# Expert steps in two parts, each with a pair of arms of its own

## The chip, the cores and the metric

The kernel runs on one core of a Trainium2 chip. Its engines are TensorE (PE: products, and PEld for the loads of weights ahead of them), VectorE (DVE), ScalarE (ACT), GpSimd (POOL) and SyncE (SP, which issues most of the DMAs). Each engine has an instruction stream of its own, read by a sequencer (PEldq, ACTq, DVEq, SPq in the rows); the streams meet by semaphores. The metric is the device time of one execution in microseconds, as the median of the runs.

## The reference, cut to what matters

Three layers follow each other. The experts at the end are what the change touches; the two ahead of them are only named here.

```python
def reference(**kwargs):
    ...
    attn_out = _attn_ref(**attn_kwargs)      # 4 x 8 heads, 576 tokens, D = 64
    x = ...                                  # 2304 tokens x 512
    x = _moe_ref(x=x, **moe_kwargs)          # relu(x @ w_in) ** 2 @ w_out, 512 -> 2048 -> 512
    return _moe2_ref(x=x, **moe2_kwargs)

def _moe2_ref(x, expert_emb, tau, w1, w2):
    ...
    expert_idx = np.argmax(logits, axis=1)   # one of 8 experts for each token
    ...
    for e in range(E):
        mask = expert_idx == e
        if not mask.any():
            continue
        h = np.maximum(x[mask] @ w1[e], 0.0)            # 512 -> 1024
        out[mask] = gate_w[mask, None] * (h @ w2[e])    # 1024 -> 512
    return out.astype(np.float32)
```

Which tokens belong to which expert is known only on the chip, at run time.

## The kernel before, in words

Attention comes first, then the dense layer, then the routing, which sorts the tokens by expert into blocks of 128 and writes a table: which expert each step uses, and some words whose bit s-1 holds a flag of step s. Then come the experts, from about 720 us on.

**Steps.** The experts run in steps of 256 tokens (two blocks), all for one expert. The program holds NST = 17 of them; steps 0 to 8 always run, later ones only while there are tokens left (L1342 to L1345). With these inputs 11 run, 0 to 10. Every product is made of three in fp32r, with hi and lo parts of both operands, so a step has 152 products on TensorE: four groups of layer 1 with 24 products each (`layer1(g)`, into a bank psh, L1249), four groups of layer 2 with 12 each (`layer2(g)`, into psy, L1265 to L1267), and 8 transposes of the tokens of the next step (`turned`, pst, L965). The order is that at the end of `body` (L1269 to L1291). Behind each layer1 group ScalarE writes hh (L1251) and VectorE hl (L1252), which layer2 of the group reads. The second half of a layer2 group stands under a small If on the word "half" (L1257), which skips it in a last, half-filled step.

**Weights.** An expert's weights are 8 pieces: 0 to 3 of w1, 4 to 7 of w2. SyncE loads them raw into x1[j] (L992 and L995; tile x in the rows), ScalarE casts a piece into Wh (L110) and VectorE computes the rest into Wl (L111). There are two slots of Wh and Wl, and a new expert takes the slot that the expert before it doesn't use. `own(j)` casts pieces 4 to 7 of the step's expert, `ahead(j)` pieces 0 to 3 of the next step's, each under an If on whether the expert changes there.

**Arms.** The slot of a step is known only at run time. So `arms` (L1293 to L1301) writes the body twice, once for slot 0 and once for slot 1, under an If and an Else on the step's bit of the word "odd"; TensorE, ScalarE and VectorE each choose on their own, by two ALU operations and a compare-and-branch (L1296 in the rows). An engine that takes the first arm ends it with a jump over the second. The choice falls to slots 0, 1, 1, 0, 0, 1, 1, 0, 0, 1 in steps 1 to 10. Within the arms the order on TensorE, ScalarE and VectorE is as written.

**Around the arms.** `block(s)` issues, behind the arms: the loads of pieces 4 to 7 on SyncE under an If on the word "more" (L1313), those of pieces 0 to 3 under another (L1316), and the gathers of the tokens of step s + 2 on POOL (L1205). `store` then multiplies psy by the gate on VectorE (L1326) and scatters the rows on POOL (L1327). In the rows, "issue" is idle time that no semaphore explains.

Of the kernel before, what the change touches and what calls it, by code (L numbers as in the profile page):

```python
# [19 lines left out]
ENG = mybir.EngineType  # L20
# [595 lines left out]
class Mlp:  # L616
# [46 lines left out]
    def layer1(self, hf, cc, f):  # L663
        nc, st, sh = self.tc.nc, self.st, self.sh
        if f == 0 and self.at == 0:
            later, self.later = self.later, at_once
            self.split_chunk(hf, cc)
            self.later = later
        xh, xl = self.xs[cc]
        self.turns += 1  # L670
        if self.psr is not None and self.turns % 2:
            ps = self.psr.tile([128, 512], F32, name="ps", tag="xt", bufs=2)
        else:
            ps = self.psm.tile([128, 512], F32, name="ps", tag="L1", bufs=1)
        ops = []
        for kc in range(4):
            fo = (f % 2) * 512 + kc * 128
            wh = sh.Wh[hf][f // 2][:, fo:fo + 128]
            wl = sh.Wl[hf][f // 2][:, fo:fo + 128]
            ops += [(wh, xh[kc]), (wh, xl[kc]), (wl, xh[kc])]  # L680
        for n, (a, b) in enumerate(ops):
            nc.tensor.matmul(ps[:, :CH], a, b, start=n == 0, stop=n == len(ops) - 1)  # L682
        r = st.tile([128, CH], F32, name="r", tag="r")
        gh = st.tile([128, CH], F32R, name="gh", tag="gh")
        gl = st.tile([128, CH], F32R, name="gl", tag="gl")
        self.later(1, "act", lambda: nc.scalar.activation(r, ps[:, :CH], AF.Relu))  # L686
        if self.square is nc.scalar:
            self.later(1, "act", lambda: nc.scalar.activation(r, r, AF.Square))
        else:
            self.later(2, "dve", lambda: nc.vector.tensor_tensor(r, r, r, ALU.mult))  # L690
        self.later(3, "act", lambda: nc.scalar.copy(gh, r))  # L691
        self.later(3, "dve", lambda: nc.vector.tensor_tensor(gl, r, gh.bitcast(F32), ALU.subtract))  # L692
        self.gT[hf, cc, f] = (gh, gl)
# [480 lines left out]
def experts(tc, sh, gates, w1, w2, out):  # L1174
    nc = tc.nc
    T = sh.T
    with ExitStack() as ctx:
# [36 lines left out]
        words = {}  # L1214

        def new(s):

            return words["once"] if s == 1 and "change" not in words else bit(words["change"], s)

        def load(js, s):  # L1220

            ev = nc.values_load(T.meta[0:1, s:s + 1], engines=[ENG.SP], min_val=0, max_val=E - 1)
            for j in js:
                load_expert_dyn(nc, sh, j, w1, w2, ev)

        def body(s, slot):


            Wh, Wl = sh.Wh[slot], sh.Wl[slot]
            hT = {}  # L1230

            def own(j):
                if s:
                    with tc.If(new(s) > 0):
                        piece(nc, sh, slot, j)

            def ahead(*js):
                if s + 1 < NST:
                    with tc.If(new(s + 1) > 0):
                        for j in js:  # L1240
                            piece(nc, sh, 1 - slot, j)

            def layer1(g):
                ps = new_bank().rearrange("p (a b) -> p a b", a=2)
                for a in range(2):
                    sl = slice((2 * g + a) * 128, (2 * g + a) * 128 + 128)
                    for kc in range(4):
                        for j, (w, x) in enumerate(((Wh, hi), (Wh, lo), (Wl, hi))):
                            nc.tensor.matmul(ps[:, a], w[kc][:, sl], x[:, kc], start=kc + j == 0, stop=kc + j == 5)  # L1249
                hh, hl = hT[g] = new_hh(), new_hl()  # L1250
                nc.scalar.activation(hh, ps, AF.Relu)  # L1251
                nc.vector.scalar_tensor_tensor(hl, ps, 0.0, hh.bitcast(F32), ALU.max, ALU.subtract)  # L1252

            def layer2(g):
                hh, hl = hT[g]
                for h in range(2):
                    with tc.If(bit(words["half"], s) < 1) if s and h else nullcontext():  # L1257
                        half(g, h, hh, hl)

            def half(g, h, hh, hl):  # L1260

                for a in range(2):
                    wh, wl = Wh[4 + g][:, a * 512:a * 512 + 512], Wl[4 + g][:, a * 512:a * 512 + 512]
                    xh, xl = hh[:, a, h * 128:h * 128 + 128], hl[:, a, h * 128:h * 128 + 128]
                    nc.tensor.matmul(y[h], xh, wh, start=g + a == 0, stop=False)  # L1265
                    nc.tensor.matmul(y[h], xh, wl, start=False, stop=False)  # L1266
                    nc.tensor.matmul(y[h], xl, wh, start=False, stop=g + a == 4)  # L1267

            own(4)  # L1269
            layer1(0)  # L1270
            own(5)
            layer1(1)
            own(6)
            own(7)
            if s == 0:
                words["once"] = nc.values_load(T.once[0:1], engines=[ENG.Activation, ENG.DVE], min_val=0, max_val=1)
            ahead(0)
            ahead(1)
            layer2(0)
            layer2(1)  # L1280
            layer1(2)
            ahead(2)
            layer1(3)
            ahead(3)
            layer2(2)
            if s + 1 < NST:
                for h in range(2):
                    turned(nc, sh, pst[h], h)
            if s == 0:
                next(gates)  # L1290
            layer2(3)  # L1291

        def arms(s, flag, *does):  # L1293

            kept = [list(r) for r in rings]
            with tc.If(bit(words[flag], s) < 1) as cmp, tc.manual_schedule(engines=IN_ORDER | {ENG.PE}):  # L1296
                does[0]()
            for r, was in zip(rings, kept):
                r[:] = was
            with cmp.Else(), tc.manual_schedule(engines=IN_ORDER | {ENG.PE}):  # L1300
                does[1]()  # L1301

        def block(s):
            if s == 0:
                body(0, 0)
                words["odd"] = word(0, [ENG.PE, ENG.Activation, ENG.DVE])
                words["change"] = word(1, [ENG.Activation, ENG.DVE])
                words["more"] = word(2, [ENG.SP])
                words["half"] = word(3, [ENG.PE])
            else:  # L1310
                arms(s, "odd", lambda: body(s, 0), lambda: body(s, 1))
            if s:
                with tc.If(bit(words["more"], s) > 0):  # L1313
                    load(range(4, 8), s)
            if s + 1 < NST:
                with tc.If(bit(words["more"], s + 1) > 0):  # L1316
                    load(range(4), s + 1)
            gather(s + 2)
# [132 lines left out]
```

## Time and profile before

| | |
|---|---|
| median of 3 runs | 982.22 us (979.92 to 982.36) |
| the profiled execution's own time | 982.79 us |
| its span, first to last instruction | 981.0 us |
| mean granted TensorE clock | 0.975 |
| busy: VectorE / ScalarE / POOL | 617.7 / 530.0 / 282.3 us |
| code fetched by DMA in the whole execution (q8) | 65 packets, 1.06 MB |

The span is that of the profiled execution; 982.79 - 981.0 = 1.8 us lie around it. TensorE's share stands with the other rows below. [...] Rows of a line give the count, the shortest, median and longest duration in ns, and the first and last start; where durations are far apart, single windows tell which one was long. A row of a window has its start and end, its length, the busy time (and count) of PE, PEld, DVE, ACT and POOL, the granted clock, the busy share of the DMA engines and GB/s. Sequencer operations (ALU, compare, branch) aren't counted as busy time; they show up only as rows of their line, and as idle time of the engine where the sequencer comes late.

### The profile page before, as it was taken

What the parts mean: (1) busy time and instruction counts of PE and PEld (TensorE: products, weight loads), DVE (VectorE), ACT (ScalarE), POOL (GpSimd) and SP (SyncE); (2) the same over time, 40 slices, a digit from 0 to 9 for tenths busy, and PEclk for the clock granted to TensorE, in tenths of its full rate; (3) what the DMA queues carried; (4) which work ended last, traced back from release to release, by engine and by line L of the source; (5) the groups of instructions that cost most, each with busy time, mean ns of one, the idle gap of its engine ahead of it and who ended that gap; (6) DMA issues with size and microseconds to landing.
All of it is one profiled execution on the core that took longest, in us unless ns stands there. A gap on an engine that the chain in (4) does not pass through costs nothing.

```text
span 981.0 us, 19093 instructions
## 1 busy us (share of the span) xinstructions
PE 919.5 (94%) x6271; PEld 791.1 (81%) x6271; DVE 617.7 (63%) x1761; ACT 530.0 (54%) x1387; POOL 282.3 (29%) x351
## 2 busy tenths in 40 slices
PE   7887788799999999999999999999999999999983
PEld 6666666688888888898888988888899889988963
DVE  4697778756676665488617778889753535353651
ACT  3676677677676766576655555665322323232430
POOL 4363554533333443000211111442312211111111
PEclk8899989899999999999999999999999999999997
DMA  7566655454444430155311112411062526252611
GB/s 167 134 175 152 155 141 133 102 127 96 115 96 116 96 87 2 65 169 155 108 44 44 64 46 90 157 66 54 22 216 66 195 85 185 88 161 85 180 40 34
DMA packets 107080, 105.79 MB, mean 108 GB/s; under 512 B 66095, under 2 KB 76335, under 8 KB 106944
## 3 DMA queue, kind: packets, MB, share of 16 engines
q1 hardware_dynamic: 101200, 90.17, 33.3%
q0 software_dynamic: 4544, 13.67, 4.4%
q8 instruction: 65, 1.06, 0.4%
q14 instruction: 71, 0.58, 0.2%
q10 hardware_dynamic: 1200, 0.30, 0.2%
HBM read 70.80 MB, written 14.70 MB: 87 GB/s over the span
## 4 chain that ended last, share of the span: by engine, by line
PE 74%; DVE 9%; issue 7%; DMA 4%; ACT 3%; POOL 2%; SPq 1%; POOLq 0%; ACTq 0%; DVEq 0%
PE ps L682 17%; PE psh L1249 11%; PE y L716 6%; PE y L718 5%; PE y L717 5%; PE xo L532 4%; PE ps L433 4%; PE pt L399 4%; PE psy L1267 3%; PE psy L1265 3%; PE psy L1266 3%; DMA raw<-in_moe_w_in_dram 2%; PE pt L401 2%; PE xo L511 1%; DVE x L819 1%
## 5 line engine op out<-in xcount | busy, mean ns | idle before, releaser
L682 PE MATMUL ps<-xh,Wh 128*128 128x256 f32 x416 | 120.0, 288 | 0.0
L394 POOL TENSOR_SCALAR A<-A,sm,g 128x512 f32<-128x512 f32 (+4 forms) x108 | 75.4, 706 | 152.0 <-DVE sm L457 58.2
L682 PE MATMUL ps<-xl,Wh 128*128 128x256 f32 x416 | 118.2, 284 | 0.9 <-DVE xl L656 0.9
L682 PE MATMUL ps<-xh,Wl 128*128 128x256 f32 x416 | 117.9, 283 | 0.0
L716 PE MATMUL y<-Wh,gh 128*128 128x512 f32 x288 | 115.3, 400 | 0.0
L718 PE MATMUL y<-Wh,gl 128*128 128x512 f32 x288 | 113.7, 395 | 0.1
L717 PE MATMUL y<-Wl,gh 128*128 128x512 f32 x288 | 113.4, 394 | 0.0
L1251 ACT ACTIVATE hh<-psh 128x512 fp32r<-128x512 f32 x44 | 26.3, 598 | 154.5 <-PE psh L1249 102.0
L1249 PE MATMUL psh<-xTh,Wh 128*128 128x256 f32 x352 | 101.0, 287 | 9.0 <-issue 8.8
L448 ACT ACTIVATE A<-A,nm 128x256 f32<-128x256 f32 (+2 forms) x144 | 80.2, 557 | 38.5 <-DVE nm L440 37.5
L1249 PE MATMUL psh<-xTl,Wh 128*128 128x256 f32 x352 | 99.9, 284 | 0.0
L1249 PE MATMUL psh<-xTh,Wl 128*128 128x256 f32 x352 | 99.9, 284 | 0.0
L440 DVE CUSTOM_DVE_ANT_0 A<-ps,mask 64x256 f32<-64x256 f32 (+4 forms) x160 | 75.5, 473 | 36.9 <-PE ps L433 34.4
L692 DVE TENSOR_TENSOR gl<-r,gh 128x256 fp32r<-128x256 f32 x144 | 69.8, 485 | 44.2 <-ACT gh L691 39.6
L1252 DVE SCALAR_TENSOR_TENSOR hl<-psh,hh 128x512 fp32r<-128x512 f32 x44 | 30.4, 690 | 103.8 <-ACT hh L1251 46.3
L686 ACT ACTIVATE r<-ps 128x256 f32<-128x256 f32 x144 | 54.8, 380 | 75.2 <-PE ps L682 67.6
L682 PEld LDWEIGHTS ps<-xh,Wh 128*128 128x128 f32 x416 | 79.6, 191 | 4.7 <-issue 1.9
L682 PEld LDWEIGHTS ps<-xl,Wh 128*128 128x128 f32 x416 | 79.7, 192 | 3.7 <-DVE xl L656 1.1
L682 PEld LDWEIGHTS ps<-xh,Wl 128*128 128x128 f32 x416 | 79.8, 192 | 0.0
L691 ACT CAST gh<-r 128x256 fp32r<-128x256 f32 x144 | 58.4, 406 | 37.4 <-PE y L717 35.3
L1249 PEld LDWEIGHTS psh<-xTh,Wh 128*128 128x128 f32 x352 | 67.6, 192 | 12.2 <-issue 11.5
L1249 PEld LDWEIGHTS psh<-xTl,Wh 128*128 128x128 f32 x352 | 67.6, 192 | 0.6
(330 smaller groups left out, 2440.1 us busy)
## 6 DMA issues: line engine op xcount, KB each, us to landing
x<-in_moe_w_dram SPq DMA_DIRECT2D x48, 512.0 KB, 5.0
raw<-in_moe_w_in_dram SPq DMA_DIRECT2D x16, 512.0 KB, 4.6
raw<-in_moe_w_out_dram SPq DMA_DIRECT2D x16, 512.0 KB, 3.8
ks<-hk SPq DMA_DIRECT2D x60, 128.0 KB, 2.4
x2d<-x SPq DMA_DIRECT2D x18, 256.0 KB, 2.0
kn<-in_k_dram SPq DMA_DIRECT2D x32, 128.0 KB, 3.7
vn<-in_v_dram SPq DMA_DIRECT2D x32, 128.0 KB, 3.2
x2p<-x SPq DMA_DIRECT2D x16, 256.0 KB, 2.5
```

What stands on the lines that cost most here:

```text
L394: nc.gpsimd.tensor_scalar(A, A, a, b, ALU.mult, ALU.mult)
L399: nc.tensor.transpose(out, A, ident)
L440: nc.vector.tensor_tensor_reduce(A[rows, a:n], tiles[j][rows, :w], mask[rows, end - w:end], -1.0, 3e38, ALU.add, ALU.min, nm[rows, j:j + 1])
L448: nc.scalar.activation(A[:, a:a + w], src, AF.Exp, bias=nm[:, 0:1], scale=sign, accum_out=sm[:, i:i + 1])
L682: nc.tensor.matmul(ps[:, :CH], a, b, start=n == 0, stop=n == len(ops) - 1)
L686: self.later(1, "act", lambda: nc.scalar.activation(r, ps[:, :CH], AF.Relu))
L691: self.later(3, "act", lambda: nc.scalar.copy(gh, r))
L692: self.later(3, "dve", lambda: nc.vector.tensor_tensor(gl, r, gh.bitcast(F32), ALU.subtract))
L716: nc.tensor.matmul(y, gh[:, sl], wh, start=first, stop=False)
L717: nc.tensor.matmul(y, gh[:, sl], wl, start=False, stop=False)
L718: nc.tensor.matmul(y, gl[:, sl], wh, start=False, stop=last)
L1249: nc.tensor.matmul(ps[:, a], w[kc][:, sl], x[:, kc], start=kc + j == 0, stop=kc + j == 5)
```

## The change

`body` gets a parameter `part`. Part 0 holds layer1(0), layer1(1), layer2(0), layer2(1) with own(4) to own(7), ahead(0) and ahead(1): 72 products. Part 1 holds the rest: layer1(2), layer1(3), layer2(2), the 8 transposes and layer2(3): 80 products. From step 1 on each part stands in a pair of arms of its own, so there are two choices on the word "odd" in each step, and the loads of pieces 4 to 7 are written between the two.

```diff
--- before.py
+++ after.py
@@ -1223,7 +1223,7 @@
             for j in js:
                 load_expert_dyn(nc, sh, j, w1, w2, ev)
 
-        def body(s, slot):
+        def body(s, slot, part):
 
 
             Wh, Wl = sh.Wh[slot], sh.Wl[slot]
@@ -1266,18 +1266,20 @@
                     nc.tensor.matmul(y[h], xh, wl, start=False, stop=False)
                     nc.tensor.matmul(y[h], xl, wh, start=False, stop=g + a == 4)
 
-            own(4)
-            layer1(0)
-            own(5)
-            layer1(1)
-            own(6)
-            own(7)
-            if s == 0:
-                words["once"] = nc.values_load(T.once[0:1], engines=[ENG.Activation, ENG.DVE], min_val=0, max_val=1)
-            ahead(0)
-            ahead(1)
-            layer2(0)
-            layer2(1)
+            if part == 0:
+                own(4)
+                layer1(0)
+                own(5)
+                layer1(1)
+                own(6)
+                own(7)
+                if s == 0:
+                    words["once"] = nc.values_load(T.once[0:1], engines=[ENG.Activation, ENG.DVE], min_val=0, max_val=1)
+                ahead(0)
+                ahead(1)
+                layer2(0)
+                layer2(1)
+                return
             layer1(2)
             ahead(2)
             layer1(3)
@@ -1302,16 +1304,17 @@
 
         def block(s):
             if s == 0:
-                body(0, 0)
+                body(0, 0, 0)
+                body(0, 0, 1)
                 words["odd"] = word(0, [ENG.PE, ENG.Activation, ENG.DVE])
                 words["change"] = word(1, [ENG.Activation, ENG.DVE])
                 words["more"] = word(2, [ENG.SP])
                 words["half"] = word(3, [ENG.PE])
             else:
-                arms(s, "odd", lambda: body(s, 0), lambda: body(s, 1))
-            if s:
+                arms(s, "odd", lambda: body(s, 0, 0), lambda: body(s, 1, 0))
                 with tc.If(bit(words["more"], s) > 0):
                     load(range(4, 8), s)
+                arms(s, "odd", lambda: body(s, 0, 1), lambda: body(s, 1, 1))
             if s + 1 < NST:
                 with tc.If(bit(words["more"], s + 1) > 0):
                     load(range(4), s + 1)
```

No computation changes its place on any engine. TensorE's stream shows what does. The first place is the middle of step 2, in the arm for slot 0, behind the last product of layer2(1); Wh0 and Wl0 are the weights of slot 0, Wh1 and Wl1 those of slot 1, psh0 to psh2 and psy0, psy1 the banks of the two layers. Before:

```order
L1265 MATMUL psy1_9341<-Wh0_5_76,hh1_9344 128x512
L1266 MATMUL psy1_9341<-Wl0_5_84,hh1_9344 128x512
L1267 MATMUL psy1_9341<-Wh0_5_76,hl1_9346 128x512
L1257 UNCONDITIONAL_BRANCH x2
L1249 MATMUL psh1_9336<-xTh_8044,Wh0_0_71 128x256
L1249 MATMUL psh1_9336<-xTl_8045,Wh0_0_71 128x256
L1249 MATMUL psh1_9336<-xTh_8044,Wl0_0_79 128x256
```

After:

```order
L1266 MATMUL psy1_9341<-Wl0_5_84,hh1_9344 128x512
L1267 MATMUL psy1_9341<-Wh0_5_76,hl1_9346 128x512
L1257 UNCONDITIONAL_BRANCH x2
L1249 MATMUL psh2_9337<-xTh_8044,Wh1_0_5674 128x256
L1234 UNCONDITIONAL_BRANCH
L1249 MATMUL psh2_9337<-xTl_8045,Wh1_0_5674 128x256
L1249 MATMUL psh2_9337<-xTh_8044,Wl1_0_5682 128x256
```

Before, layer1(2) of the same arm comes next, still with Wh0 (psh1, the third group's bank). Now the arm ends here with a jump, and layer1(0) of the arm for slot 1 stands behind it, with Wh1 (L1234 is the empty If of `own`).

The second place is the end of that arm for slot 1, the middle of step 2, where the new choice stands (L1298 is the line of L1296 in the changed file):

```order
L1266 MATMUL psy1_9341<-Wl1_5_5687,hh1_9344 128x512
L1267 MATMUL psy1_9341<-Wh1_5_5679,hl1_9346 128x512
L1257 UNCONDITIONAL_BRANCH x2
L1315 UNCONDITIONAL_BRANCH
L1298 REGISTER_ALU x2
L1298 COMPARE_AND_BRANCH
L1249 MATMUL psh1_9336<-xTh_8044,Wh0_0_71 128x256
L1249 MATMUL psh1_9336<-xTl_8045,Wh0_0_71 128x256
L1249 MATMUL psh1_9336<-xTh_8044,Wl0_0_79 128x256
```

What was the next row of one arm is now reached over a jump, two ALU operations and a compare-and-branch.

The third place is the end of step 2 and the choice of step 3 on TensorE. Before:

```order
L1266 MATMUL psy1_9341<-Wl1_7_5689,hh1_9344 128x512
L1267 MATMUL psy1_9341<-Wh1_7_5681,hl1_9346 128x512
L1257 UNCONDITIONAL_BRANCH x2
L1313 UNCONDITIONAL_BRANCH
L1316 UNCONDITIONAL_BRANCH
L1296 REGISTER_ALU x2
L1296 COMPARE_AND_BRANCH
L1249 MATMUL psh0_9335<-xTh_8044,Wh0_0_71 128x256
```

After:

```order
L1266 MATMUL psy1_9341<-Wl1_7_5689,hh1_9344 128x512
L1267 MATMUL psy1_9341<-Wh1_7_5681,hl1_9346 128x512
L1257 UNCONDITIONAL_BRANCH x2
L1319 UNCONDITIONAL_BRANCH
L1298 REGISTER_ALU x2
L1298 COMPARE_AND_BRANCH
L1249 MATMUL psh0_9335<-xTh_8044,Wh0_0_71 128x256
```

The choice stands where it stood; the empty branch of the loads' If (L1313) has left this place. From the choice of step 2 to that of step 3 the stream has 326 rows before and 330 after; the second choice cuts the 330 in two, behind 165. A row of a product is two instructions, its weight load and the product.

On SyncE the same step, around the last load of pieces 4 to 7 and the first of pieces 0 to 3. Before:

```order
L995 ISA
L995 DMA x1_7_4700<-in_moe2_w2_dram 128x2x512
L1313 UNCONDITIONAL_BRANCH x2
L1316 REGISTER_ALU x2
L1316 COMPARE_AND_BRANCH
L1222 TENSOR_LOAD meta_9226
```

After:

```order
L995 ISA
L995 DMA x1_7_4700<-in_moe2_w2_dram 128x2x512
L1315 UNCONDITIONAL_BRANCH x2
L1298 UNCONDITIONAL_BRANCH
L1249 UNCONDITIONAL_BRANCH x2
L1319 REGISTER_ALU x2
L1319 COMPARE_AND_BRANCH
L1222 TENSOR_LOAD meta_9226
```

The loads and their order are the same; three empty branches, those of the arms of the second part, have come between them. Each load waits for the same reads of its buffer on ScalarE and VectorE as before. ScalarE and VectorE get the same second choice as TensorE, at the same place of the step.

## Rows read from the trace of the kernel before

**Rows 1.** Page: busy us (share of the span) xinstructions

```profile
PE 919.5 (94%) x6271; PEld 791.1 (81%) x6271; DVE 617.7 (63%) x1761; ACT 530.0 (54%) x1387; POOL 282.3 (29%) x351
```

**Rows 2.** Waits of TensorE, 720 to 981 us: us in total, times, longest

```profile
PE psh L1249 <- issue: 8.8, 5, 4.5
```

**Rows 3.** Chain: start us, us, what; last row timeline of TensorE

```profile
770.72 1.86 issue
...
796.29 0.26 issue
...
820.26 5.65 PE psh L1249 x48
...
843.42 5.66 PE psh L1249 x48
...
866.59 1.94 issue
...
868.53 7.47 PE psh L1249 x48
...
893.75 0.29 issue
...
945.41 0.58 PE L1249 MATMUL psh<-xTh,Wh 128*128 128x256 f32 x1 [4.49 <-issue]
```

**Rows 4.** L1296: ns min/median/max, starts; whole execution, then windows

```profile
L1296 PEldq COMPARE_BRANCH  x10: 68/1710/4788, 721.6 to 941.4; - x10
...
L1296 DVEq COMPARE_BRANCH  x10: 43/56/80, 725.8 to 941.2; - x10
...
L1296 PEldq COMPARE_BRANCH  x1: 4712/4712/4712, 767.8 to 767.8; - x1
...
L1296 PEldq COMPARE_BRANCH  x1: 3331/3331/3331, 793.2 to 793.2; - x1
...
L1296 PEldq ALU_OP  x2: 36/36/36, 840.2 to 840.3; - x2
...
L1296 PEldq COMPARE_BRANCH  x1: 68/68/68, 840.4 to 840.4; - x1
...
L1296 PEldq COMPARE_BRANCH  x1: 3970/3970/3970, 941.4 to 941.4; - x1
```

**Rows 5.** Line L1257, the same columns

```profile
L1257 PEldq COMPARE_BRANCH  x76: 65/169/383, 727.9 to 963.5; - x76
```

**Rows 6.** Windows: span, busy us (count), PEclk; code: packets, MB

```profile
442.00:640.00 198.00, 197.66 (x1279) 176.27 (x1278) 141.12 (x429) 114.26 (x291) 38.30 (x59) 1.00 0.26 88
...
q8 instruction: 11, 0.18, 0.4%
...
723.00:945.40 222.40, 213.57 (x1389) 192.54 (x1387) 98.02 (x157) 70.87 (x129) 39.45 (x37) 0.99 0.40 128
...
q8 instruction: 23, 0.38, 0.7%
```

**Rows 7.** Windows over 49 products after two gaps, columns as in rows 6

```profile
868.60:875.90 7.30, 7.30 (x49) 7.30 (x50) 2.53 (x5) 1.63 (x3) 1.93 (x2) 0.77 0.41 131
...
945.40:952.50 7.10, 7.09 (x49) 7.09 (x50) 1.89 (x3) 1.63 (x3) 0.99 (x1) 0.80 0.04 15
```

**Rows 8.** Windows over steps 2 and 8, columns as in rows 6

```profile
747.40:770.70 23.30, 23.30 (x155) 20.96 (x152) 11.73 (x21) 8.84 (x16) 8.70 (x8) 1.00 0.49 166
...
894.10:917.50 23.40, 23.40 (x152) 21.20 (x153) 10.05 (x16) 8.85 (x16) 4.08 (x4) 1.00 0.39 127
```

**Rows 9.** SyncE: a row of its waits from 720 us, one of its timeline

```profile
SPq L995 <- DVE Wl L111: 42.5, 16, 5.7
...
773.52 9.33 SPq L995 DMA_DIRECT2D x<-in_moe_w_dram  x4
```

**Rows 10.** Timeline at the end of the program

```profile
965.48 0.40 PE L1267 MATMUL psy<-Wh,hl 128*128 128x512 f32 x1
...
971.55 0.99 POOL L1327 DMA_INDIRECT out_dram<-x,idxs  x1 [2.83 <-DMA out_dram<-x,idxs]
```

## The prediction, made before the changed kernel was run

> **What bounds the kernel now.** I read the engine shares first [rows 1]: TensorE is busy for 94% of the span, so time is won only where it stands still or runs slowly. The change lies in the experts stage, from about 720 us on, so I asked for TensorE's waits there. There is one kind [rows 2]: the first product of a step (psh, L1249) waits for "issue", 8.8 us over 5 places. No semaphore, no DMA and no other engine ends these waits. The chain shows four of the places, 1.86, 0.26, 1.94 and 0.29 us, and the timeline the fifth, 4.49 us [rows 3]; a step takes some 23 us and step 5 begins at 820.26, so they stand ahead of steps 3, 4, 7, 8 and 10. Their sum is 8.84 us.
>
> The cause is one line further up in the queue. At each step TensorE's sequencer chooses its arm at L1296. Ten choices took 68 to 4788 ns [rows 4]. Five are long, and they are those of the same five steps: three stand in the rows, at 767.8, 793.2 and 941.4 us with 4712, 3331 and 3970 ns [rows 4]; that of step 7 is the longest, 4788. The sequencer runs ahead of the array, by 770.72 - 767.8 = 2.9 us at step 3; 4.7 - 2.9 = 1.8 us remains visible, which is the gap of 1.86 us. At step 4 the 3.3 us are covered but for 0.26.
>
> Why does the same branch take 68 ns or 4.7 us? The small branches of L1257, which jump over a dozen instructions, took at most 383 ns in 76 cases [rows 5], so a branch as such doesn't stall. What differs is distance: an arm is 152 products and as many weight loads, and with the branches about 320 instructions. Code comes by DMA in pieces: from 442 to 640 us, where nothing jumps far, 11 packets of code of 0.18 MB came (16 KB each) while TensorE ran 1279 products and 1278 loads [rows 6], 2557 / 11 = 232 instructions for a packet (some may be for other engines, so rather more than fewer). From 723 to 945.4 us 23 packets came for 2776 instructions [rows 6], one for 121: the arms not run are fetched too. A jump over 320 instructions is longer than a packet and can leave one out; one over fewer than 232 ends in the same packet or the next. That the stall waits for such a packet is my reading of these counts; no row shows the wait itself. Alignment matters as well: step 6 jumped over as much as step 10 and took 68 ns (840.4 us) [rows 4].
>
> [...]
>
> **The change part by part.** (a) Shorter arms. They become 72 and 80 products: 144 and 160 products and loads, with branches about 155 and 170. No jump over an arm reaches a packet's 232. If so, the five stalls go. Two of the five, at steps 4 and 8, didn't jump over an arm but fell through right behind a step that had run its second arm; their visible part is 0.26 + 0.29 us. I keep 0.3 us of gaps as left over: 8.84 - 0.3 = **8.5 us** won. Bounds: nothing of them goes (0), or all (8.84).
>
> (b) What follows the gaps. [...] Steps 5 and 6, without a gap ahead, take 23.16 and 23.17 us (from start to start less the next gap [rows 3]). Steps 3, 4 and 7 take 23.70, 23.71 and 25.22 [rows 3], and step 8's window shows 23.4 us of products without a pause, so 23.5 with its edges [rows 8]: an excess of 0.5, 0.5, 2.0 and 0.3 over 23.2. Step 10's first 49 products cost 7.1 - 5.7 = 1.4 more. Together 4.7 us. Where no gap opens, the clock has no reason to fall in steps 7 and 10 (3.2 us of the 4.7). The 0.5 of steps 3, 4 and 8 comes at a full clock and I can't explain it; they are just the steps behind a stall, so I take it as a consequence. I count **4.5 us** won; bounds 0 and 4.7.
>
> (c) Ten more choices on TensorE. Each is two ALU operations (they start 0.2 us ahead of the branch at the earliest) and a branch of 68 ns where it doesn't stall [rows 4], and one more jump at the end of an arm (a small branch's median is 169 ns [rows 5]): with room to spare 0.5 us, ten of them 5 us on the sequencer. In the middle of the step the products queued are those of layer 2, as at the end, where the lead is 2.9 us; it hides 0.5 us five times over. Without that cover it would be 5 us. I take **0**; what a stall there would cost is the first two rivals' matter.
>
> (d) The same choices on ScalarE and VectorE: the branch takes 43 to 80 ns on VectorE [rows 4], with its two ALU operations some 0.2 us. Both are busy for less than half of a step of 23 us (8.84 and 11.73 us in step 2) [rows 8] and TensorE waits for neither [rows 2]. VectorE's choice stands behind the casts of the pieces and ahead of layer1(2)'s hl, which waits for TensorE anyway. Cost 0; if all of it lay on the path, ten times 0.2 us.
>
> (e) The loads of pieces 4 to 7. In the program they move ahead of the second choice, but SyncE computes nothing in an arm, only empty branches: the order of its DMAs is the same, and each still waits for VectorE's last read of its buffer (L995 <- DVE Wl, 42.5 us over 16 waits) [rows 9]. It is that read, not the place in the program, that starts them: the first came at 773.52 us, 1.0 us into step 3, so already within what becomes the first part. Three more empty branches a step on SyncE, if they cost as much as VectorE's, add 0.2 us where it waits for tens. POOL's gathers and scatters keep their order. TensorE has no wait on a load in this stage [rows 2]. Cost and gain **0**. The transfers do move earlier with the steps, by up to 13 us over the stage, and all by about the same.
>
> (f) The tail. Behind TensorE's last product come VectorE's multiply and two scatters, the last at 971.55 us, held by the landing of the one before [rows 10]; all of it follows TensorE at a fixed distance and moves with it.
>
> **Sum.** 982.79 (profiled execution, span 981.0) - 8.5 - 4.5 = 969.8. The median of the runs is 982.22, 0.57 lower, so 969.2. All of both bounds: 982.22 - 13.5 = 968.7.
>
> **The rivals.** First, half of the stalls stay: alignment decides, as the 68 ns at step 6 and the 3970 at step 10 show, and a choice in the middle of a step may find its code missing too. Twice as many choices, each with a shorter wait that the lead of 2.9 us covers in part. Half of both terms lost: 982.2 - 6.5 = 975.7; with a fourth kept, 979. For it: step 4's stall without a long jump. Against: no jump is as long as a packet, and the small jumps have no stall in 76.
>
> Second, the slower side: the stall belongs to the choice between arms (a compare on a run-time word, whose outcome the fetch can't know), not to the distance. Half of the ten choices stalled, 8.84 us visible, 0.88 us for a choice. Ten more in the middle, with the same lead, add 8.8 us, and with the slow stretch behind them (4.7) up to 13.5: 991 to 996. It decides as soon as more stalls arise in the middle than go at the step starts. For it: the choice at 793.2 us stalls on falling through. Against: L1257's compares are run-time choices too and never stall.
>
> Third, the gaps go but the 0.5 us a step and the clock's loss don't: 982.2 - 8.5 = 973.7. For it: nothing shows why steps 3, 4 and 8 are slower at a full clock. Against: the clock's part follows the gaps.
>
> Fourth, the change does nothing: as to the loads that is my reading of (e); as to the arms it would need stalls moved to equal places, 982.
>
> **How the numbers follow.** Forecast (nearly all gaps and what follows them gone, 968 to 972): 0.66. Third rival, 973.7: 0.07. First rival, 975 to 979: 0.13. No change: 0.06. Slower: 0.08. A measurement of this kernel tells about 0.3% (3 us) from no change; so faster 0.86, same 0.06, slower 0.08. The range runs from 966.0 (the upper bound of the gain, 968.7, less the 2.3 us by which the fastest run lies below the median, with a little kept) to 977.5, in the first rival: outside lie no change, slower, and the end of the first rival, under 2 in 10.
>
> **What would show it.** Right: TensorE's waits for issue in the stage 0.6 us or less in sum; twenty choices on its sequencer, nearly all under 100 ns; steps of 23.2 us throughout; granted clock 1.00 at the start of steps 7 and 10; the loads of pieces 4 to 7 still about 1 us into the step behind VectorE's casts. Wrong: choices of 3 us and more in the middle of steps, with gaps before the psh of layer1(2); or no gaps and yet steps of 23.7. The forecast falls if packets hold fewer instructions than an arm, or if a choice loses the code at hand whatever its distance.

## The result, and the profile after

| | before | changed |
|---|---|---|
| median of the runs taken side by side | 981.62 us (979.92 to 982.36, 4 runs) | 970.64 us (969.43 to 971.12, 4 runs) |
| profiled execution | 982.79 us, span 981.0 | 970.91 us, span 969.2 |
| TensorE's waits for "issue" in the experts | 8.84 us at 5 places | 1.36 us at 2 places |

The ratio is 0.9889, with a 95% interval of 0.9872 to 0.9906: 11.0 us faster. Forecast were 969.2 us and 13.0 us of gain, with a range of 966.0 to 977.5. Sign and range held; the gain is 2 us smaller, and three of the sum's terms were off, which the experiments explain.

TensorE's waits from 715 us on, in the changed kernel (line, what ended the wait, us in total, times, longest); they answer to [rows 2]:

```profile
PE psh L1249 <- issue: 1.4, 2, 1.0
PE psh L1249 <- PEq L1257: 0.7, 1, 0.7
PE psh L1249 <- DVE Wl L111: 0.2, 1, 0.2
```

The first row is what is left of the 8.8 us. The other two are new: the kernel before has no such wait. The timeline shows the four places; the two for issue stand ahead of steps 3 and 7, the other two in the middle of steps 9 and 10:

```profile
770.30 0.39 PE L1249 MATMUL psh<-xTh,Wh 128*128 128x256 f32 x1 [0.99 <-issue]
...
864.12 0.39 PE L1249 MATMUL psh<-xTh,Wh 128*128 128x256 f32 x1 [0.37 <-issue]
...
923.18 0.38 PE L1249 MATMUL psh<-xTh,Wl 128*128 128x256 f32 x1 [0.22 <-DVE Wl L111]
...
944.45 0.39 PE L1249 MATMUL psh<-xTh,Wh 128*128 128x256 f32 x1 [0.69 <-PEq L1257]
```

The choices on TensorE's sequencer (L1298 is L1296 of before; whole execution, then the two long ones, then two stretches), against [rows 4]:

```profile
L1298 PEldq COMPARE_BRANCH  x20: 65/155/3936, 720.2 to 944.0; - x20
...
L1298 PEldq COMPARE_BRANCH  x1: 3936/3936/3936, 766.3 to 766.3; - x1
...
L1298 PEldq COMPARE_BRANCH  x1: 3313/3313/3313, 860.8 to 860.8; - x1
...
L1298 PEldq COMPARE_BRANCH  x2: 220/276/333, 778.3 to 790.9; - x2
...
L1298 PEldq COMPARE_BRANCH  x4: 68/68/68, 814.3 to 848.5; - x4
```

There are three kinds: 65 to 93 ns, 217 to 443 ns, and two of more than 3 us.

The prediction said that no row shows what a long choice waits for. The packets of TensorE's code (DMA queue q8, 16 KB each) show it. In the kernel before, a packet runs inside each of the five long choices, for instance from 865.98 to 866.99 us in that of step 7 (863.68 to 868.47 us), here in the window 864 to 869:

```profile
q8 instruction: 1, 0.02, 1.3%
```

Each of the five choices ends 1.3 to 1.5 us behind the landing of its packet; the changed kernel's two end 1.27 and 1.50 us behind theirs (768.98 and 862.57 us). Over the experts in all thirteen traces of this case, each of the 36 branches that took over 2 us has a packet landing in it and ends 1.0 to 1.6 us behind the last one; of the 1235 that took under 0.5 us, 9 have one. So the long choices wait for code.

Steps 7 and 10 now start at a granted clock of 1.00 (full speed), where they had 0.77 and 0.80. The windows over their first 49 and 50 products (columns as in [rows 6]) answer to [rows 7]:

```profile
864.10:870.00 5.90, 5.88 (x49) 5.88 (x50) 4.20 (x7) 1.63 (x3) 2.24 (x2) 1.00 0.60 195
...
934.80:940.50 5.70, 5.70 (x50) 5.70 (x49) 4.50 (x7) 1.63 (x3) 1.39 (x2) 1.00 0.37 106
```

Where the time went, by steps, from one step's first product to the next one's (step 10: to its last product):

| step | 1 | 2 | 3 | 4 | 5 | 6 | 7 | 8 | 9 | 10 | sum |
|---|---|---|---|---|---|---|---|---|---|---|---|
| before, us | 24.02 | 25.27 | 23.96 | 23.55 | 23.16 | 25.27 | 25.51 | 23.56 | 27.81 | 20.07 | 242.18 |
| changed, us | 24.01 | 24.40 | 23.52 | 23.44 | 23.16 | 23.70 | 23.54 | 23.44 | 23.63 | 19.30 | 232.14 |

The sum falls by 10.0 us. The spans differ by 11.8; 1.4 of that lies ahead of the experts (their first product starts at 694.1 us instead of 695.5, with the same program up to there) and 0.3 behind them, which is scatter between two executions. So the change itself is worth 10.0 us in the traces, against the 13.0 of the sum.

### The profile page after: what moved, and what is told of

Same layout as the page of the kernel before. It is cut to its first block, busy times and chain, and to the rows that moved or that the text cites. A ratio compares the mean times of both kernels' runs of the same rounds, so it can differ in the third digit from the quotient of the medians.

```text
span 969.2 us, 19247 instructions
## 1 busy us (share of the span) xinstructions
PE 915.1 (94%) x6271; PEld 787.8 (81%) x6271; DVE 618.4 (64%) x1761; ACT 529.8 (55%) x1387; POOL 282.5 (29%) x351
## 4 chain that ended last, share of the span: by engine, by line
PE 76%; DVE 7%; issue 6%; DMA 4%; ACT 3%; POOL 2%; SPq 1%; ACTq 0%; POOLq 0%; DVEq 0%
PE ps L682 18%; PE psh L1249 11%; PE y L716 6%; PE y L718 6%; PE y L717 6%; PE xo L532 5%; PE ps L433 5%; PE pt L399 4%; PE psy L1267 3%; PE psy L1265 3%; PE psy L1266 3%; PE pt L401 2%; DMA raw<-in_moe_w_in_dram 2%; PE xo L511 1%; DVE x L819 1%
## 5 line engine op out<-in xcount | busy, mean ns | idle before, releaser
L1265 PE MATMUL psy<-Wh,hh 128*128 128x512 f32 x168 | 67.0, 399 | 0.1
```

## The experiments

Three theories were open. **A**: code comes in blocks, and a jump waits when it lands in a block that is not there yet; what counts is how many borders of blocks are passed, and how fast one behind the other. **B**, the prediction's reading: the distance of the jump counts. **C**: every choice between arms costs at some rate.

For A the places can be counted. In straight code (kernel before) packets of code started at 522.98, 542.95, 562.45, 581.82 and 601.50 us, and 256, 254, 256 and 258 instructions started between them. Over all 13 intervals from 442 to 699 us the counts run from 232 to 290, with a mean of 257. I take a block as 256 instructions, the mean of the four counts; that is an estimate. With borders at that spacing every jump of every kernel below can be looked up, by the position of its instructions in TensorE's compiled program. In the changed kernel, from step 2 to 3, two jumps with two ALU operations between them lead from instruction 10898 to 11069 and from 11071 to 11226, and pass the borders at 10945 and 11201: 3936 ns. From step 6 to 7 they lead from 13498 to 13826, past 13505 and 13761: 3313 ns. From step 9 to 10 the same pair of jumps leads from 15448 to 15777 and passes only the border at 15553: 220 ns.

The count holds widely. The kernel before, the changed one, e1, e2, e3, e5, e6, e8 and the repeats e10 and e11 below have 130 jumps over an arm, at its start or from the end of the other one (two with no product between them taken as one). With borders at 10945 and every 256 from there, 26 pass two or three borders, and all 26 wait, 3.1 to 6.4 us. The other 104 pass one or none; 102 of them take at most 457 ns. The two that wait (2.7 us, step 10 in e8 and its repeat) have passed one more border some ten instructions ahead of the jump. The spacing comes from the packets. No row shows the exact place: with all borders moved by 4 down to 25 up the exceptions stay at 3 or fewer; elsewhere there are 4 to 26.

### e1_shift56: the same code, 56 instructions further on

```diff
-STRICT, BUSY = 9, {-5: 14, 0: 12, 2: 6}
+STRICT, BUSY = 9, {-5: 14, 0: 12, 2: 6, 3: 28}
```

> The kernel before with 28 more dummy transposes on TensorE (56 instructions) in a pause of 3.8 us near 13 us, which shifts all later code on TensorE by some 56 instructions and changes nothing else. Theory A (a jump waits when it lands in a block of code that is still being fetched, so what counts is where it crosses the borders of blocks of some 256 instructions): the stalls move. By a count of borders with 3.4 us for a block and a lead of 28 instructions, TensorE's pauses in the experts go from 7.6 (8.84 measured) to 12.2 us: about 0.8 in step 1 or 2, 2.9 at step 3, none at 4 and 8, 0.8 at step 6, 3.4 at step 7, 4.1 at step 10; total time +4 to +7 us with the slow clock behind the long ones. Theory B (the distance: a taken choice over 320 instructions waits, wherever it lies): the same five pauses, 8.8 us, no change of the time. Theory C (each choice between arms waits at some rate): no change.

Measured: 985.65 us against 982.17, ratio 1.0039 (1.0021 to 1.0058); the 3.5 us lie just below A's 4 to 7. The waits in total, the places, then the line of the small branches, which also holds the jump at the end of a first arm, and the choices (whole execution, and that of step 4):

```profile
PE psh L1249 <- issue: 11.8, 6, 4.1
```

```profile
770.03 0.38 PE L1249 MATMUL psh<-xTh,Wh 128*128 128x256 f32 x1 [2.03 <-issue]
...
773.26 0.37 PE L1249 MATMUL psh<-xTl,Wh 128*128 128x256 f32 x1 [1.78 <-issue]
...
845.44 0.38 PE L1249 MATMUL psh<-xTh,Wh 128*128 128x256 f32 x1 [0.53 <-issue]
...
870.25 0.38 PE L1249 MATMUL psh<-xTh,Wh 128*128 128x256 f32 x1 [1.38 <-issue]
...
873.23 0.28 PE L1249 MATMUL psh<-xTh,Wh 128*128 128x256 f32 x1 [2.01 <-issue]
...
946.80 0.58 PE L1249 MATMUL psh<-xTh,Wh 128*128 128x256 f32 x1 [4.09 <-issue]
```

```profile
L1257 PEldq COMPARE_BRANCH  x76: 65/169/3894, 724.6 to 965.0; - x76
...
L1296 PEldq COMPARE_BRANCH  x10: 68/257/4885, 718.4 to 943.1; - x10
...
L1296 PEldq COMPARE_BRANCH  x1: 430/430/430, 795.1 to 795.1; - x1
```

Nothing changed but the place of the code, and the pauses moved as A's count said: none ahead of steps 4 and 8, a new one ahead of step 6, 3.8 and 3.4 us in two pieces at steps 3 and 7. (The one expected in step 1 or 2 is 0.41 us, where TensorE's products of the gates come first.) B and C said "no change". Two rows speak against them. The choice of step 4 leads over 321 instructions as before and takes 430 ns instead of 3331: so distance alone makes no wait. And an unconditional jump over an arm, which cost at most 383 ns before ([rows 5]), now waits 3.9 us: so it is not the choice that waits.

### e2_shift112: some 113 instructions further on

```diff
-STRICT, BUSY = 9, {-5: 14, 0: 12, 2: 6}
+STRICT, BUSY = 9, {-5: 14, 0: 12, 2: 6, 3: 28, 9: 28}
```

> The same with 56 more dummy transposes (28 near 13 us, 28 near 35 us): code shifted by some 113 instructions. Theory A: pauses in the experts fall to 3.5 us (0.8 to 1.0 in steps 1, 3 and 7, 0.7 at step 10), none long enough for the clock to fall: total time -5 to -7 us without touching the arms. Theory B: the same five pauses, 8.8 us, no change. Theory C: no change.

Measured: 979.03 us against 982.17, ratio 0.9976 (0.9955 to 0.9997). The waits, the choice of step 3, and the code fetched from 766 to 773 us:

```profile
PE psh L1249 <- issue: 6.4, 3, 3.5
...
L1296 PEldq COMPARE_BRANCH  x1: 6413/6413/6413, 766.2 to 766.2; - x1
```

```profile
q8 instruction: 2, 0.03, 3.7%
```

The places are A's (steps 3, 7 and 10; 4 and 8 are gone; the one expected in step 1 doesn't show as a pause), and without touching the arms the kernel is faster, though by 3.1 us and not by 5 to 7, with an interval that ends just short of no change. The sizes aren't A's: 6.4 us instead of 3.5. At step 3 the choice took 6.4 us, with two packets in that time instead of the one that the count gave it. A's account of places holds; its sizes are good to about 3 us.

### e3_arms_swapped: slot 1's arm first

```diff
-            with tc.If(bit(words[flag], s) < 1) as cmp, tc.manual_schedule(engines=IN_ORDER | {ENG.PE}):
+            with tc.If(bit(words[flag], s) > 0) as cmp, tc.manual_schedule(engines=IN_ORDER | {ENG.PE}):
...
-                arms(s, "odd", lambda: body(s, 0), lambda: body(s, 1))
+                arms(s, "odd", lambda: body(s, 1), lambda: body(s, 0))
```

> The kernel before with the two arms in the other order: slot 1 first, slot 0 behind it. Steps 1 to 10 use slots 0, 0, 1, 1, 0, 0, 1, 1, 0, 1 if the casts ahead of steps 3, 5, 7, 9 and 10 are read rightly. Theory A: pauses of 5.8 us in all, in steps 2 (3.1), 5, 6, 8 and 9 (0.4 to 1.0 each), and none at 3, 4, 7 and 10; total -2 to -4 us. Theory B: the taken choices are now those of slot 0, so five pauses at steps 1, 2, 5, 6 and 9. Theory C: pauses stay at 3, 4, 7, 8 and 10. If the pace of 233 instead of 228 ns for a psy product belongs to slot 1 and not to the pauses or to the second arm, it stays in steps 3, 4, 7 and 8.

Measured: 981.07 us against 982.17, ratio 0.9991 (0.9973 to 1.0009); the change of the total is not clear of zero, and A's 2 to 4 us of gain didn't come. The waits in total (A: 5.8) and the places:

```profile
PE psh L1249 <- issue: 7.4, 4, 3.0
...
749.27 0.58 PE L1249 MATMUL psh<-xTh,Wh 128*128 128x256 f32 x1 [3.01 <-issue]
...
823.17 0.38 PE L1249 MATMUL psh<-xTh,Wh 128*128 128x256 f32 x1 [2.10 <-issue]
...
848.59 0.38 PE L1249 MATMUL psh<-xTh,Wh 128*128 128x256 f32 x1 [0.44 <-issue]
...
920.75 0.39 PE L1249 MATMUL psh<-xTh,Wh 128*128 128x256 f32 x1 [1.87 <-issue]
```

These are steps 2, 5, 6 and 9, four of the five that A named (step 8 was to have 0.4 and has none). All pauses of before, at 3, 4, 7, 8 and 10, are gone: C falls. A and B each named one step too many. That of B is step 1, which takes the second arm here: its jump over 319 instructions took 457 ns (at 720.4 us), so B in its strict form falls too.

The run bears on two more things. First, the order of the slots. It can be read from the casts: the pieces of a next expert are cast in steps 2, 4, 6, 8 and 9 of the kernel before, for instance here, from 747 to 770 us and from 917 to 941:

```profile
L110 ACT CAST Wh<-x x10: 610/618/622, 754.5 to 769.6; 128x512 fp32r<-128x512 f32 x10
...
L110 ACT CAST Wh<-x x17: 610/619/624, 916.4 to 939.8; 128x512 fp32r<-128x512 f32 x17
```

So the expert changes at steps 3, 5, 7, 9 and 10, and steps 1 to 10 use slots 0, 0, 1, 1, 0, 0, 1, 1, 0, 1. The order given with the kernel before (0, 1, 1, 0, 0, 1, 1, 0, 0, 1) was wrong. Second, the pace: the 24 products of layer2(0) and (1) take 5.60 us in steps 3, 4, 7 and 8 and 5.48 in steps 1, 2, 5, 6 and 9, in the kernel before, in the changed one, in e1, e2 and here, where the pauses lie elsewhere and slot 1 runs in the first arm. The slower pace goes with slot 1, not with a pause or with the second arm; why slot 1 costs 5 ns a product was not tried.

### e4_cut_140_12: the cut elsewhere, the long jump back

```diff
                 layer2(0)
                 layer2(1)
+                layer1(2)
...
+                layer2(2)
...
                 return
-            layer1(2)
...
             layer2(3)
```

> The changed kernel with the cut at another place: the first part is everything up to the transposes (140 products, some 295 instructions an arm), the second is layer2(3) alone (12 products). As many choices as in the changed kernel, but the long jump is back. Theory A: pauses of 14.4 us, 1 to 2.4 us in each of steps 2, 3, 4, 6, 7, 8, 9 and 10; total 5 to 14 us more than the kernel before. Theory B: five pauses as in the kernel before, the short jumps add none: 982. Theory C: twice as many choices as before, 9 to 14 us more than before as well, but with pauses ahead of both parts.

Measured: 970.80 us against 982.17, ratio 0.9894 (0.9867 to 0.9921): as good as the changed kernel, though an arm is again some 295 instructions long. The waits, and the choices of the whole execution and around steps 3 and 10:

```profile
PE psh L1251 <- issue: 1.2, 3, 0.5
PE psy L1267 <- ACT xTh L110: 0.6, 1, 0.6
```

```profile
L1300 PEldq COMPARE_BRANCH  x25: 68/215/3710, 719.7 to 951.5; - x25
...
L1300 PEldq COMPARE_BRANCH  x3: 73/2655/2685, 762.7 to 766.6; - x3
...
L1300 PEldq COMPARE_BRANCH  x3: 83/2325/3710, 927.4 to 932.3; - x3
```

All three expectations missed. B's 982 falls: the long jump is there and the time is not lost. C's falls too. A's 14.4 us came from a count that left out the second half of layer 2 in every step; a new count gives 2.5 us, but it was made with the result known and proves nothing. The lesson is in the rows. The sequencer still stalls, two times 2.7 us at step 3, but now 12 products (2.8 us) lie between the two stalls, and the products in the queue cover nearly all of each. In the kernel before, single stalls were covered the same way (3331 ns at step 4, all but 0.26 us); what cost was what followed each other with no product between: 4.7 us at step 3, and at step 10 first 3.4 us between two records of the sequencer (937.80 to 941.19, with a packet landing at 939.70), then the choice of 3970 ns, of which 4.49 us show.

### e5_ahead_late: ahead(0) and ahead(1) in the second part

```diff
-                ahead(0)
-                ahead(1)
                 layer2(0)
                 layer2(1)
                 return
+            ahead(0)
+            ahead(1)
             layer1(2)
```

> The changed kernel with ahead(0) and ahead(1) moved from the end of the first part to the start of the second. Theory: the pauses of 0.22 us (step 9, at 923.18) and 0.69 us (step 10, at 944.45) in the middle of steps of the changed kernel are a wait that the cut added: layer1(2) of one slot waits for the casts that ahead would make into the same slot in the other arm of the first part, since the order of arms is not known across two pairs. Moved, nothing in the second part reads what the first part's other arm may write; both pauses go, about 1.0 us in steps 9 and 10, total 969.6, while the pauses at steps 3 and 7 (1.4 us) stay. Rival (the pauses belong to the second choice of TensorE itself, or to code that comes late): they stay, 970.6.

Measured: 970.32 us against 982.91, ratio 0.9874 (0.9850 to 0.9898). The waits:

```profile
PE psh L1249 <- issue: 1.5, 2, 1.0
PE psh L1249 <- PEq L1257: 0.7, 1, 0.7
```

Half right. The total can't tell it from the changed kernel; from first to last product of the experts it is 259.56 us against 259.93. The wait in step 9 is gone (layer1(2) and (3) take 5.66 us there instead of 6.14), so the cut had added it: in the changed kernel the first products of layer1(2) carry waits for the casts of the first part, because ahead in the *other* arm of the first part writes the slot that they read, and the two pairs of arms are not known to choose alike. VectorE's casts there ran from 918.23 to 923.13 us, and the product started at 923.18. The 0.69 us in step 10 stays: it is the sequencer's. In this half-filled step the second half of layer 2 is left out, the last operation of L1257 on the sequencer comes at 943.8 us, and the choice behind it, here in the changed kernel, finds no queue to hide in:

```profile
L1298 PEldq COMPARE_BRANCH  x1: 443/443/443, 944.0 to 944.0; - x1
```

No run was made on that last reading; e9, with its cuts elsewhere, doesn't have this wait.

### e6_load_behind: the loads back behind the arms

```diff
+                arms(s, "odd", lambda: body(s, 0, 1), lambda: body(s, 1, 1))
                 with tc.If(bit(words["more"], s) > 0):
                     load(range(4, 8), s)
-                arms(s, "odd", lambda: body(s, 0, 1), lambda: body(s, 1, 1))
```

> The changed kernel with the loads of pieces 4 to 7 back behind both pairs of arms. Theory: the place of the loads counts for nothing, since each waits for VectorE's read of its buffer: loads about 1 us into the step as before, total as the changed kernel, 970.6. Rival (the earlier place starts transfers earlier and is part of the gain): some us slower, loads later by up to half a step.

Measured: 971.55 us against 982.91, ratio 0.9897 (0.9870 to 0.9924), the experts' stage 259.93 us from first to last product, as in the changed kernel (259.93). The first of these loads, here and in the changed kernel:

```profile
771.39 8.18 SPq L995 DMA_DIRECT2D x<-in_moe_w_dram  x4
```

```profile
772.10 8.90 SPq L995 DMA_DIRECT2D x<-in_moe_w_dram  x4
```

Step 3 starts at 769.22 us here and at 770.30 in the changed kernel: 2.2 and 1.8 us into the step, in both later than the 1 us of before. The loads' place shows no effect on the time.

### e7_three_parts and e9_three_parts_60_36_56: three pairs of arms

e7, cut to its core:

```diff
-                ahead(0)
-                ahead(1)
+                return
+            if part == 1:
                 layer2(0)
                 layer2(1)
+                layer1(2)
                 return
-            layer1(2)
+            ahead(0)
+            ahead(1)
+            layer1(3)
             ahead(2)
-            layer1(3)
             ahead(3)
             layer2(2)
...
                 arms(s, "odd", lambda: body(s, 0, 0), lambda: body(s, 1, 0))
+                arms(s, "odd", lambda: body(s, 0, 1), lambda: body(s, 1, 1))
...
-                arms(s, "odd", lambda: body(s, 0, 1), lambda: body(s, 1, 1))
+                arms(s, "odd", lambda: body(s, 0, 2), lambda: body(s, 1, 2))
```

> Three pairs of arms a step: layer1(0) and (1) (48 products), then layer2(0), (1) and layer1(2) (48), then the rest (56), with all of ahead in the third part. Theory A (blocks of code): two jumps in a row now pass over some 220 instructions, at most one border of a block, so no pause is left at any shift of the code: 0 us of pauses instead of 1.4, no wait in the middle of the step, about 2.4 us less than the changed kernel, 968.2. Theory C (each choice costs): 10 more choices, 4 to 9 us slower than the changed kernel. Rival: the casts of ahead come late on VectorE and hold layer2(3) or the next step's start by some tenths of a us each.

Measured: 1007.84 us against 982.91, ratio 1.0259 (1.0234 to 1.0284). All expectations missed: the rival named VectorE, but tenths of a us. It is not code that costs:

```profile
PE psy L1267 <- DVE x L1335: 13.9, 3, 4.6
PE psy L1267 <- DVE room L1335: 11.4, 4, 2.9
```

```profile
782.60 0.77 PE L1267 MATMUL psy<-Wh,hh 128*128 128x512 f32 x1 [4.62 <-DVE x L1335]
```

```profile
779.30 2.48 DVE L111 TENSOR_TENSOR Wl<-x,Wh 128x512 fp32r<-128x512 f32 x4
781.71 0.74 DVE L1335 TENSOR_SCALAR x<-psy,gate 128x512 f32<-128x512 f32 x1
```

The waits for issue are gone altogether, as A said. But seven steps wait 2.8 to 4.6 us for VectorE: the second multiply of the step before (L1335) now stands behind the first part's casts on VectorE, because nothing in the first part touches psy any more; and layer2(0) must wait for it. e9 puts one line back (its edit against e7):

```diff
+                layer2(0)
                 return
             if part == 1:
-                layer2(0)
                 layer2(1)
```

> e7_three_parts with layer2(0) back in the first part (60, 36 and 56 products). In e7 the second multiply of the psy of the step before came behind the first part's casts on VectorE, since nothing in the first part read psy, and layer2(0) waited 2.8 to 4.6 us for it in seven steps; with layer2(0) in the first part both multiplies stand ahead of the choice again. Theory A (blocks of code): one stall of 2.7 us of the sequencer at step 3 and one at step 10, both covered, pauses of 0 to 0.4 us in all, 967 to 969. Theory C (each choice costs): 30 choices, slower than the changed kernel by 4 to 9 us. If e7's loss wasn't the multiplies' place, 1000 and more again.

Measured: 968.81 us against 981.24, ratio 0.9884 (0.9860 to 0.9908). The waits:

```profile
PE psy L1267 <- ACT Wh L110: 0.5, 1, 0.5
PE psh L1251 <- issue: 0.5, 1, 0.5
```

As A said, 967 to 969 us. Thirty choices and 0.5 us of waiting for code: C is out.

### e8_ahead_late_shift112, and the changed kernel beside it

```diff
-STRICT, BUSY = 9, {-5: 14, 0: 12, 2: 6}
+STRICT, BUSY = 9, {-5: 14, 0: 12, 2: 6, 3: 28, 9: 28}
...
-                ahead(0)
-                ahead(1)
                 layer2(0)
                 layer2(1)
                 return
+            ahead(0)
+            ahead(1)
```

> e5_ahead_late with 56 more dummy transposes as in e2_shift112, which shift TensorE's code by some 113 instructions. Theory A: the two stalls at steps 3 and 7 need two borders passed in a row; shifted, they don't occur: pauses of 0 to 0.3 us (step 10), about 1.2 us less than e5_ahead_late, 968.3. Rival (the stalls at steps 3 and 7 belong to the change from the first arm of one step to the second of the next, wherever the code lies): pauses of 1.4 us as in the changed kernel.

Measured: 968.46 us against 982.91, ratio 0.9858 (0.9837 to 0.9879). Of TensorE's waits one is left; the choices of the whole execution stand below it:

```profile
PE psh L1249 <- PEq L1257: 0.7, 1, 0.7
...
L1298 PEldq COMPARE_BRANCH  x20: 71/157/2769, 718.7 to 940.4; - x20
```

The stalls at steps 3 and 7 went with the place of the code, so they didn't belong to the change from arm to arm. One choice of 2769 ns is left, at step 10; the queue covers all of it. A last set ran it again beside the changed kernel and e9 on one chip.

> The changed kernel itself, beside the two other versions of this set on the same chip: 970.6, ratio to the kernel before 0.989.

> e8_ahead_late_shift112 again, beside the changed kernel on the same chip: some 2 us less than the changed kernel, ratio to the kernel before 0.986 to 0.987, if the two pauses at steps 3 and 7 and the wait in step 9 (1.36 + 0.5 us) are what it saves.

Measured: the changed kernel 970.99 us, ratio 0.9900 (0.9879 to 0.9921); the shifted one 968.74, ratio 0.9872 (0.9849 to 0.9895); e9 0.9884. From first to last product of the experts the traces have 259.93, 257.84 and 258.47 us. So the shifted version saves 2.1 us in the traces, as expected; the medians agree with it (2.2), but the intervals of the two ratios overlap, so the times alone don't prove it. By the traces it beats the changed kernel, by the times only the one before.

## Why the prediction was right, and where it wasn't

**The bound and the place** were right: TensorE in the experts' stage, five pauses at the step starts, made by the sequencer. 7.5 of the 8.84 us went.

**Step (a), "No jump over an arm reaches a packet's 232. If so, the five stalls go"**, failed in part: three places went, two stayed with 1.36 us, where 0.3 were kept. The 232 is a slip: the 11 packets from 442 to 640 us stand at both ends of the window, so 2557 instructions lie in ten intervals, 256 each. And one jump was looked at; but where a step in slot 0 is followed by one in slot 1 two come in a row, and 171 + 155 instructions can pass two borders. What is at hand at a jump no row shows; past at most one border 102 of 104 jumps took at most 457 ns, past two or three all 26 waited 3.1 to 6.4 us, and of the two waits here each has a packet landing in it (768.98 and 862.57 us). Nor was the length of the arm needed (e4): what the cut bought is that the fetches no longer come close behind each other with nothing to cover the second.

So the prediction's distance counts, but by way of the borders. As an estimate from the block of 256: a pair of before (322 + 321) passes at least two borders wherever it lies, a pair of the changed kernel in some 28% of places, a single jump of before in some 25%, one of the changed kernel never. The changed kernel lay badly in two of its three pairs. How large the gain comes out is in part the luck of the place: the same shift gave the kernel before -3.1 us (e2) and the cut one -1.9 (e5 to e8).

The remark that the choice at 793.2 us falls through, and that step 6 jumped over as much as step 10, rested on the wrong order of slots. With the right one all five long choices of before jump over a first arm, and the five of 68 to 89 ns fall through. So what the prediction put forward for its first two rivals, a stall without a long jump, is not in the trace.

**Term (b), 4.5 us for what follows the gaps.** The clock's part came as forecast: step 7's first 48 products take 5.94 us instead of 7.47, at a granted clock of 1.00 instead of 0.77, and step 10's 1.35 us less, at 1.00 instead of 0.80: 2.9 of 3.2 (7.47 - 5.66 and 7.1 - 5.7 [rows 3, 7]). The 0.5 of steps 3, 4 and 8, "just the steps behind a stall, so I take it as a consequence", was the wrong step: 1.3 us were booked and some 0.3 came. Two things were in it. Slot 1's pace, which e3 showed: steps 4 and 8 take 23.44 us in the changed kernel without a pause ahead, the slot 0 step 5 23.16. And a misreading: steps 3 and 4 were counted from their first products, but up to rows of the chain, which lie 0.16 us behind the point where a next product can start (820.26 against 820.10 for step 5). They came out as 23.70 and 23.71 us; like for like they take 23.54 and 23.55. The third rival had it right there.

**Terms (c) and (d).** The ten added choices cost TensorE nothing wherever a queue hid them, as said. The terms left out that the cut adds waits: TensorE waited for nothing but code before, and the prediction went by that, but layer1(2) got new waits for the casts, 0.48 us in step 9 (e5), and a choice behind the left-out half in step 10 costs 0.55 (its first 12 layer 2 products span 4.05 us instead of 3.50). Together 1.0 us, where 0 stood; the bound given for (c), 5 us, covers it, but its reason was another.

**Terms (e) and (f)**, loads and tail, were right in the cost: e6 shows no difference, and the tail is the same but for 0.3 us.

**The sum again:** 7.5 + 2.9 + 0.3 - 1.0 = 9.7 of the 10.0 us measured in the stage.

**The signs.** Of those that the prediction named for being right, the clock of 1.00 in steps 7 and 10 came. The others didn't: waits for issue of 1.36 us and not 0.6, ten choices of 217 ns to 3.9 us where nearly all were to be under 100 ns (the ten that take the second arm), steps 2 to 9 of 23.2 to 24.4 us, loads 1.8 us into step 3.

**The rivals.** The slower one, a stall for each choice, fell three times (e3, e4, e9). The first, stalls that stay for reasons of alignment, was the true mechanism, with a smaller share than "half" (1.36 of 8.84 us), and not in the middle of a step.

## What to carry to other kernels

Where an engine waits for "issue" at a choice between large pieces of code, count the jumps that follow each other without work between them, and how many blocks of code they pass: a few products between two jumps did as much here as shorter arms (e4, 0.9894 against 0.9889), and a shift of the code on top of shorter arms took the last stalls out of sight (e8, 0.9858, against 0.9874 for e5); a shift alone did little (e2, 0.9976). Before a body is cut at such a choice, look for what is then ordered by a wait or falls out of order: a buffer written in one arm and read in the other's next part (e5), a multiply that no longer precedes its reader's part (e7). And when a trace shows two kinds of steps, find out from the data which step is which before a reason is built on it.

## What was not expected of the hardware

A shift of TensorE's code by 56 or 113 instructions, with the same work, moved the whole kernel by +0.4 and -0.2%. And a pause's length alone doesn't fix what the clock does: in the stretch behind 1.94 us the mean granted clock was 0.77 ([rows 7], step 7), with 0.50 from 869.8 to 873.1 us, behind 1.87 us 1.00 (e3, step 9), and in e2 behind 2.62 us 1.00, behind 3.47 us 0.76. The windows over some 48 products behind the two pauses of e2:

```profile
772.70:779.90 7.20, 7.20 (x48) 7.20 (x49) 1.86 (x3) 1.62 (x3) 0.99 (x1) 0.76 0.36 122
870.30:876.00 5.70, 5.70 (x48) 5.70 (x49) 1.91 (x4) 1.62 (x3) 1.32 (x2) 1.00 0.53 154
```

What decides there stays open; a fall costs some 1.4 to 1.6 us each time (48 products in 7.0 to 7.3 us instead of 5.7).
